# Attention output rows in two halves: six products in place of a step's weighted sums, twice per unit

## The chip, the cores and the metric

The kernel runs on one core of one Trainium2 chip. Its time is the device time of one execution in microseconds. TensorE is called PE below, ScalarE ACT, VectorE DVE, GpSimd POOL, and SP is the engine that issues most DMAs.

## The reference

One transformer block with parallel branches, in float32, over 2048 tokens of 448 features; 16 heads of 28 share one key head and one value head; the hidden layer has 1792 features.

```python
def _A_ref(x, wq, wk, wv, wo):
    q = (x @ wq).reshape(B, S, H, Dh).transpose(0, 2, 1, 3)
    k = x @ wk
    v = x @ wv
    scores = jnp.einsum("bhqd,bkd->bhqk", q, k) * (Dh ** -0.5)
    p = _softmax(scores, axis=-1)
    o = jnp.einsum("bhqk,bkd->bhqd", p, v)
    return o.transpose(0, 2, 1, 3).reshape(B, S, H * Dh) @ wo

def _B_ref(x, w1, b1, w2, b2):
    y = _layernorm(x, axis=-1)
    h = _gelu(jnp.einsum("bsd,df->bsf", y, w1) + b1)
    return jnp.einsum("bsf,fd->bsd", h, w2) + b2

xn = _layernorm(x, axis=-1)
return x + _A_ref(xn, wq, wk, wv, wo) + _B_ref(xn, w1, b1, w2, b2)
```

## The kernel before

The kernel goes through three stages: normalisation and the q, k, v products; the MLP branch, whose result plus `x` and the bias is parked row tile by row tile in DRAM (`ad`); and the attention, which fills the time from about 350 us to the end and is all that the change touches.

**Units and steps.** The attention is cut into 16 units `u`, each 512 queries (chunk `c`) of 4 heads (group `g`), the groups of a chunk one after the other. A unit has 16 key tiles of 128 keys, and its work is laid out in 8 steps `i`. A step holds, in the order that the string `ORDER` spells out:

- 7 or 8 **scores** (`score`, L694 and L695): a 128x512 product on PE into a tile `m` of PSUM, and the exponential from `m` into a tile `p` of SBUF on ACT. `SHARES` deals 60 of them over the 8 steps (8, 8, 8, 7, 7, 7, 7, 8); the first key tile's four blocks come another way (next point).
- in steps 3 to 6, one **maximum product** for the unit after the next (`max_job`, L523 on PE into an `m`, read out by DVE at L530), and one exponential of the next unit's first key tile (`first_exp`, L538 on ACT, from SBUF), which needs a subtraction on DVE first (`first_shift`, L535).
- pieces of the **normalisation** of the last finished unit (`norm_jobs`: copy of `po` at L807, transposes, reciprocal, product, on DVE; a subtraction on POOL), pulled from the stream `side` at the two places `n` of a step.
- at the step's end (`P`) the **weighted sums** of two key tiles (`BURST = 2`): `pv`, L880, four 32-column products per key tile side by side in the array, adding into `po`. They run one step behind the scores; what they use sits in a ring of 12 pairs of `p` tiles.

**The output rows.** When the four groups of a chunk are done, its 512 rows are multiplied with `wo`. That is spread over the next chunk's units: each unit from 4 on does one row tile of 128, `o_part`, in step 5. It is 12 products of 128x448 (4 groups, 3 products each, L767 to L769), one accumulation in one tile `m`, then one addition on DVE to the row that `load_rows_of` fetched from `ad` in step 0 (L772), and the DMA out. In that step the weighted sums are left out, and the step after does four key tiles instead of two:

```python
o_steps = {(u, 5): (u // NG - 1, u % NG) for u in range(NG, NU)}
...
if (u, i) in o_steps:
    o_part(*o_steps[u, i], range(NG))
    continue
for _ in range((BURST if n else 0) * (1 + ((u, i - 1) in o_steps))):
    pv(*pvq.pop(0))
```

**What orders the work.** Every engine runs its instructions in the order in which the program emits them; there is no scheduler. PE therefore cannot start the next scores until a burst of sums or output products is through. The tiles `m` (scores, maximum products, output rows alike) are handed out strictly in turn by `mtile`: seven of them, three from the pool `mp` and four from the pool `ring`. A product into an `m` waits until the tile handed out seven places before has been read. `po` is a single tile. The last unit ends in `pv_last` and `end_jobs`, which the change does not touch.

Of the kernel before, what the change touches and what calls it, by code (L numbers as in the profile page):

```python
# [15 lines left out]
P = 128  # L16
S, D, H, DH, F = 2048, 448, 16, 28, 1792
NT = S // P
CT = 4
NCH = NT // CT  # L20
CW = CT * P
NG = H // 4
# [18 lines left out]
def block_kernel(ctx, tc, x, wq, wk, wv, wo, w1, b1, w2, b2, out):  # L41
    nc = tc.nc
    pe, act, dve, pool = nc.tensor, nc.scalar, nc.vector, nc.gpsimd
# [11 lines left out]
    ov = out[0].rearrange("(p t) d -> p t d", t=NT)  # L55
# [54 lines left out]
    def mtile(shape):  # L110
        if rings:
            given.append(0)
            if len(given) % 7 > 3 or len(given) % 7 == 0:
                return rings[0].tile(shape, F32, name="m")
        return mp.tile(shape, F32, name="m")
# [94 lines left out]
    def bn_end(c, k0=0, n=CT):  # L210
        for k in range(k0, k0 + n):
            dve.bn_aggr(lnp[:, CT * c + k, :], sts[c][:, k, :])
        ts = slice(CT * c + k0, CT * c + k0 + n)
        r = rstd(lnr[:, ts], lnp[:, ts, 1], n)
        next(r)
        yield
        next(r)
        dve.scalar_tensor_tensor(lnb[:, ts], lnp[:, ts, 0], -1.0, lnr[:, ts], op0=ALU.mult, op1=ALU.mult)
        yield
# [9 lines left out]
    def norm_both():  # L229
        dve.tensor_mul(lnq, lnp[:, :, 1], lnr)  # L230
        dve.tensor_mul(lnq, lnq, lnr)
        r = rstd(lnq, lnq, NT)
        next(r)
        yield
        next(r)
        yield
        turned = mtile([NT, P])
        pe.transpose(turned, lnq, ident)
        rows = wp.tile([NT, P], F32, name="rows")
        dve.tensor_copy(rows, turned)  # L240
        nc.scalar.dma_start(second, rows)
        act.activation(warm, one, AF.Tanh)
        yield
# [162 lines left out]
    for c, at in ((2, ((0, 1), (0, 2), (0, 2), (0, 3))), (3, ((1, 0), (1, 1), (1, 2), (1, 3)))):  # L406
        for k in range(CT):
            later(*at[k], lambda t=CT * c + k: bn(t))
        g = bn_end(c)
        for k in range(2):  # L410
            later(c - 1, 0, lambda g=g: next(g), True)
    g = norm_both()
# [12 lines left out]
    NU = len(units)  # L425
    qss, ots = {}, {}
# [43 lines left out]
    def load_q(u, blocks=range(4)):  # L470
        c, g = units[u]
        cols = slice(c * CW, (c + 1) * CW)
        if u < 3 and 0 in blocks:
            qst.append(xt_p.tile([P, 4, CW], F32R, name="xh") if u < 2 else
                       att.tile([P, 4, CW], F32R, name="xh", bufs=1))
            pool.memset(f(qst[u]), 0.0)
        qs = qst[u % 3]
        for b in blocks:
            blk, i = ((1, 0), (2, 0), (0, 1), (3, 1))[b]
            src = qd[i][4 * DH * g:4 * DH * (g + 1), cols].rearrange("(j r) n -> r j n", r=DH)  # L480
            nc.sync.dma_start(f(qs[32 * blk:32 * blk + DH, :, :]), src)
        qss[u] = qs
# [36 lines left out]
    def max_job(u, j):  # L519
        if j == 0:  # L520
            mrs[u] = keep.tile([P, 4 * NT], F32, name="mr2", bufs=2)
        pm = mtile([P, CW])
        pe.matmul(pm, km, qss[u][:, j, :], start=True, stop=True)  # L523
        if u == 0:
            if j == 0:
                lasts.append(f(xl_p.tile([P, 4, CW], F32R, name="xl")))
            tts[u, j] = lasts[0][:, j]
        else:
            tts[u, j] = att.tile([P, CW], F32, name="tt", bufs=5)
        dve.transpose(tts[u, j], pm)  # L530
        dve.tensor_reduce(mrs[u][:, NT * j:NT * j + NT], blocks_of(tts[u, j]), axis=AX.X, op=ALU.max)
# [17 lines left out]
    def shift_jobs(u):  # L549
        for j in range(4):  # L550
            first_shift(u, j)
            yield
            first_exp(u, j)
            yield
            first_back(u, j)
# [130 lines left out]
    def score(u, kt, j):  # L686
        if not halfway:
            p = pair_of()
            halfway.append(p[:, 1])
            p = p[:, 0]  # L690
        else:
            p = halfway.pop()
        s = mtile([P, CW])
        pe.matmul(s, ks[:, kt * P:(kt + 1) * P], qss[u][:, j, :], start=True, stop=True)  # L694
        act.activation(p, s, AF.Exp, scale=SCALE)  # L695
        ps[u, kt, j] = p
# [4 lines left out]
    for n in range(len(mslots) + LAG):  # L701
        c, ft = mslots[n] if n < len(mslots) else (NCH, n - len(mslots))
        if 5 < ft < 10:
            line(CT * MLP_ORDER[c] + ft - 6)
        if 6 < ft < 11:
            a = lines[CT * MLP_ORDER[c] + ft - 7]
# [30 lines left out]
    woh = att.tile([P, NG, D], F32R, name="woh", bufs=1)  # L737
    wol = att.tile([P, NG, D], F32R, name="wol", bufs=1)

    def load_wo():  # L740
        pool.memset(wor, 0.0)
        for j in range(4):
            src = wo.rearrange("(g j d) n -> j d g n", j=4, d=DH)[j]
            nc.sync.dma_start(wor[32 * j + 1:32 * j + 1 + DH, :, :], src)

    def prep_wo(g):
        pool.tensor_scalar(woh[:, g, :], wor[:, g, :], 1.0, 0.0, op0=ALU.mult, op1=ALU.add)
        pool.tensor_sub(wol[:, g, :], wor[:, g, :], f(woh[:, g, :]))

    rows = {}  # L750

    def load_rows_of(c, tiles):
        for k in tiles:
            rows[c, k] = keep.tile([P, D], F32, name="a", bufs=4)
            dve.memset(rows[c, k][0:1, 0:1], 0.0)
            nc.sync.dma_start(rows[c, k], ad[:, CT * c + k, :])
# [3 lines left out]
    def o_part(c, k, gs):  # L760
        if gs[0] == 0:
            parts[c, k] = mtile([P, D])
        po = parts[c, k]
        ts = slice(k * P, (k + 1) * P)
        for g in gs:
            oth, otl = ots[c, g]
            pe.matmul(po, oth[:, ts], woh[:, g, :], start=(g == 0), stop=False)  # L767
            pe.matmul(po, oth[:, ts], wol[:, g, :], start=False, stop=False)  # L768
            pe.matmul(po, otl[:, ts], woh[:, g, :], start=False, stop=(g == NG - 1))  # L769
        if gs[-1] == NG - 1:  # L770
            a = rows[c, k]
            dve.tensor_add(a, a, parts.pop((c, k)))  # L772
            (nc.scalar if k % 2 and c == NCH - 1 else nc.sync).dma_start(ov[:, CT * c + k, :], a)

    def o_jobs(c):
        for k in range(CT):
            o_part(c, k, range(NG))
            yield
# [107 lines left out]
    xside = Stream()  # L886
    pvq = [(u, kt) for u in range(NU) for kt in range(NT)]
    last = NU * NT // 2 - 1
    o_steps = {(u, 5): (u // NG - 1, u % NG) for u in range(NG, NU)}
    for u in range(NU):  # L890
        todo = [(u, kt, j) for kt in range(1 if u else 2, NT) for j in range(4)]
        for i in range(NT // 2):
            n = NT // 2 * u + i
            if n >= last - 1:
                load_rows_of(NCH - 1, (range(CT - 1), [CT - 1])[n - last + 1])
            for v, step in o_steps:
                if v == u and i == 0:
                    load_rows_of(o_steps[v, step][0], [o_steps[v, step][1]])
            if n == 9:
                load_wo()  # L900
            if 12 <= n < 12 + NG:
                prep_wo(n - 12)
            if i == 0 and u + 2 < NU:
                load_q(u + 2)
            jobs = todo[:SHARES[i] if u else 8 * (i > 0)]
            todo = todo[len(jobs):]
            maxima = [(u + 2, i - 3 - (u == 0))] if 3 + (u == 0) <= i < 7 + (u == 0) else []
            if u == 0 and i in (1, 2):
                maxima = [(1, 2 * i - 2), (1, 2 * i - 1)]
            for what in ORDER:  # L910
                if what == "s" and jobs:
                    score(*jobs.pop(0))
                elif what == "M":
                    for v, j in maxima:
                        if v < NU:
                            max_job(v, j)
                elif what in "XY":
                    if what == "X" and i == (2 if u else 3) and u + 1 < NU:
                        xside.add(shift_jobs(u + 1))
                    xside.step()  # L920
                elif what == "e":
                    if i == 7 and u + 2 < NU:
                        load_max(u + 2)
                    if n == 2:
                        load_max(1)
                elif what == "n":
                    side.step()
                elif what == "o":
                    if n == last:
                        o_part(NCH - 1, 0, range(NG - 1))  # L930
                elif what == "P":
                    assert not jobs
                    if (u, i) in o_steps:
                        o_part(*o_steps[u, i], range(NG))
                        continue
                    for _ in range((BURST if n else 0) * (1 + ((u, i - 1) in o_steps))):
                        pv(*pvq.pop(0))
        assert not todo
# [85 lines left out]
```

## Time and profile before

| | us |
|---|---|
| median of 3 runs | 895.28 |
| the three runs | 895.28, 900.3, 891.72 |
| the profiled execution's own time | 891.71 |
| its span | 889.8 |

| engine | busy us (share of the span) | instructions |
|---|---|---|
| PE | 878.8 (99%) | 4914 |
| ACT | 701.9 (79%) | 1334 |
| DVE | 485.7 (55%) | 963 |
| POOL | 73.2 (8%) | 82 |

The granted TensorE clock is 1.000 over the whole span. The shares are averages over stages: the MLP is PE's alone, while in the attention ACT is busy almost all the time as well. Matmuls overlap and their ends are modelled, so PE's 99% does not say whether it has slack; that has to be read from the start times. The profile's count of sums is double the program's: one 32-column float32 product shows as two entries.

### The profile page before, as it was taken

How to read it: one execution, taken by the hardware profiler on the slowest of the kernel's cores; microseconds unless marked ns; L12 is line 12 of the kernel's file. 1: busy time of each engine (PE TensorE's matmuls, PEld its weight loads, DVE VectorE, ACT ScalarE, POOL GpSimd, SP SyncE). 2: the span in 40 equal slices, each digit the busy share in tenths (PEclk: the TensorE clock that was granted, in tenths of full speed). 3: DMA queues.
4: the chain of work that ended last, by engine and by line, in shares of the span. 5: the costliest groups of instructions: out<-in, count | busy, mean ns of one | idle time of the engine just before them, and what ended most of it. 6: DMA issues, size and time to landing. Idle time of an engine off the chain costs nothing.

```text
span 889.8 us, 13236 instructions
## 1 busy us (share of the span) xinstructions
PE 878.8 (99%) x4914; PEld 565.4 (64%) x4914; DVE 485.7 (55%) x963; ACT 701.9 (79%) x1334; POOL 73.2 (8%) x82
## 2 busy tenths in 40 slices
PE   9999999999999999999999999999999999999997
PEld 8777888888888886444444554554554554554555
DVE  6757765656556776654464463463463463463212
ACT  5777564545555457999999999999999999999992
POOL 5450000000000002040000000000000000000000
PEclk9999999999999999999999999999999999999999
DMA  9985232013003004031102202201202201200001
GB/s 293 321 263 173 83 128 83 1 72 118 1 1 105 10 11 125 2 79 43 36 8 53 64 11 53 64 11 53 63 11 53 63 11 53 63 11 13 21 31 66
DMA packets 36297, 60.69 MB, mean 68 GB/s; under 512 B 7782, under 2 KB 23348, under 8 KB 35204
## 3 DMA queue, kind: packets, MB, share of 16 engines
q1 hardware_dynamic: 34644, 58.95, 21.8%
q10 hardware_dynamic: 1584, 0.84, 0.4%
q8 instruction: 40, 0.66, 0.3%
q14 instruction: 29, 0.24, 0.1%
HBM read 39.89 MB, written 18.88 MB: 66 GB/s over the span
## 4 chain that ended last, share of the span: by engine, by line
PE 83%; ACT 8%; DVE 4%; DMA 2%; issue 1%; SPq 0%; ACTq 0%; DVEq 0%
PE m L694 25%; PE po L880 24%; PE ph L178 11%; ACT p L695 5%; PE m L627 4%; PE m L633 4%; PE m L630 4%; PE m L767 2%; PE m L523 2%; PE m L769 1%; PE m L768 1%; PE ph L181 1%; PE ph L183 1%; PE qp L178 1%; DMA raw<-in_B_w_dram 1%
## 5 line engine op out<-in xcount | busy, mean ns | idle before, releaser
L695 ACT ACTIVATE p<-m 128x512 f32<-128x512 f32 x956 | 489.9, 747 | 27.4 <-PE m L694 27.0
L694 PE MATMUL m<-xh,ks 128*128 128x512 f32 x960 | 268.8, 409 | 0.7 <-DVE tt L530 0.3
L694 PEld LDWEIGHTS m<-xh,ks 128*128 128x128 f32 x960 | 174.5, 188 | 139.7 <-ACT p L695 70.8
L880 PE MATMUL po<-p,vs 128*32 128x512 f32 x2016 | 239.9, 598 | 0.0
L880 PEld LDWEIGHTS po<-p,vs 128*32 128x32 f32 x2016 | 53.8, 109 | 119.7 <-issue 119.4
L600 ACT ACTIVATE hz<-hx,b1s 128x512 f32<-128x512 f32 x56 | 40.6, 726 | 101.7 <-DVE hx L597 101.7
L530 DVE STREAM_TRANSPOSE tt<-m 128x512 f32<-128x512 f32 x60 | 42.9, 715 | 94.9 <-PE m L523 94.9
L627 PE MATMUL m<-w2h,hh 128*128 128x448 f32 x224 | 81.9, 366 | 0.0
L633 PE MATMUL m<-w2h,hl 128*128 128x448 f32 x224 | 81.8, 365 | 0.0
L630 PE MATMUL m<-w2l,hh 128*128 128x448 f32 x224 | 81.8, 365 | 0.0
L807 DVE COPY oc<-po 128x512 f32<-128x512 f32 x15 | 10.4, 692 | 120.3 <-PE po L880 120.3
L604 DVE SCALAR_TENSOR_TENSOR hz<-hz,hx 128x512 f32<-128x512 f32 x56 | 38.8, 692 | 52.2 <-ACT hx L601 52.2
L178 PE MATMUL ph<-xh,w1h 128*128 128x512 f32 x159 | 63.1, 397 | 1.8 <-DVE hx L597 1.8
L178 PE MATMUL ph<-xh,w1l 128*128 128x512 f32 x159 | 62.3, 392 | 0.0
L178 PE MATMUL ph<-xl,w1h 128*128 128x512 f32 x159 | 62.3, 392 | 0.0
L822 POOL TENSOR_TENSOR otl<-oc,oth 128x512 fp32r<-128x512 f32 x15 | 24.1, 1608 | 463.5 <-DVE oth L820 272.3
L597 DVE TENSOR_TENSOR hx<-ph,xn 128x512 f32<-128x512 f32 x53 | 36.5, 689 | 39.5 <-PE ph L183 39.3
L538 ACT ACTIVATE tt<-tt 128x512 f32<-128x512 f32 x60 | 53.4, 890 | 0.0
L544 DVE STREAM_TRANSPOSE p<-tt 128x512 f32<-128x512 f32 x60 | 42.1, 702 | 9.4 <-ACT tt L538 9.3
L627 PEld LDWEIGHTS m<-w2h,hh 128*128 128x128 f32 x224 | 42.1, 188 | 5.0
L630 PEld LDWEIGHTS m<-w2l,hh 128*128 128x128 f32 x224 | 42.1, 188 | 4.6
L607 ACT ACTIVATE hz<-hz 128x512 f32<-128x512 f32 x56 | 35.2, 629 | 12.0 <-DVE hz L604 12.0
(173 smaller groups left out, 1040.2 us busy)
## 6 DMA issues: line engine op xcount, KB each, us to landing
xh<-qd SPq DMA_DIRECT2D x64, 224.0 KB
qd<-qe SPq DMA_DIRECT2D x24, 256.0 KB
a<-in_A_x_dram SPq DMA_DIRECT2D x20, 224.0 KB
ad<-a SPq DMA_DIRECT2D x16, 224.0 KB
a<-ad SPq DMA_DIRECT2D x16, 224.0 KB
raw<-in_B_w_dram SPq DMA_DIRECT2D x7, 448.0 KB
out_dram<-a SPq DMA_DIRECT2D x14, 224.0 KB
xd<-xh SPq DMA_DIRECT2D x2, 1024.0 KB
```

The source lines that it names most:

```text
L178: pe.matmul(ps, w, v, start=(n == 0), stop=False)
L530: dve.transpose(tts[u, j], pm)
L538: act.activation(tts[u, j], tts[u, j], AF.Exp, scale=SCALE)
L544: dve.transpose(p0s[u][:, j], tts.pop((u, j)))
L600: act.activation(hz, hx, AF.Square, bias=b1s[:, ft:ft + 1], scale=GELU[0] ** 0.5)
L604: dve.scalar_tensor_tensor(hz, hz, 1.0, hx, op0=ALU.add, op1=ALU.mult)
L627: pe.matmul(m2[k], hh[:, ts], w2h, start=(ft == 0), stop=False)
L630: pe.matmul(m2[k], hh[:, ts], w2l, start=False, stop=False)
L633: pe.matmul(m2[k], hl[:, ts], w2h, start=False, stop=(ft == NF - 1))
L694: pe.matmul(s, ks[:, kt * P:(kt + 1) * P], qss[u][:, j, :], start=True, stop=True)
L695: act.activation(p, s, AF.Exp, scale=SCALE)
L880: pe.matmul(po[32 * j:32 * j + 32, :], vs[:, kt, :], ps.pop((u, kt, j)), start=(kt == 0), stop=(kt == NT - 1))
```

## The change

A row tile's 12 products are done in two halves of six. The first half takes groups 0 and 1 and the place of the sums in step 1; the second takes groups 2 and 3 and the place of the sums in step 5. Each half is an accumulation of its own in its own tile `m`, and each is added to the row in SBUF, so there are two additions on DVE per row tile instead of one. The rows go out after the second. The steps after each, 2 and 6, do four key tiles each.

```diff
+    def o_half(c, k, gs):
+        po = mtile([P, D])
+        ts = slice(k * P, (k + 1) * P)
+        for g in gs:
+            oth, otl = ots[c, g]
+            pe.matmul(po, oth[:, ts], woh[:, g, :], start=(g == gs[0]), stop=False)
+            pe.matmul(po, oth[:, ts], wol[:, g, :], start=False, stop=False)
+            pe.matmul(po, otl[:, ts], woh[:, g, :], start=False, stop=(g == gs[-1]))
+        a = rows[c, k]
+        dve.tensor_add(a, a, po)
+        if gs[-1] == NG - 1:
+            nc.sync.dma_start(ov[:, CT * c + k, :], a)
...
-    o_steps = {(u, 5): (u // NG - 1, u % NG) for u in range(NG, NU)}
+    o_steps = {(u, 4 * h + 1): (u // NG - 1, u % NG, range(2 * h, 2 * h + 2)) for u in range(NG, NU) for h in range(2)}
...
-            for v, step in o_steps:
-                if v == u and i == 0:
-                    load_rows_of(o_steps[v, step][0], [o_steps[v, step][1]])
+            if i == 0 and u >= NG:
+                load_rows_of(u // NG - 1, [u % NG])
...
-                        o_part(*o_steps[u, i], range(NG))
+                        o_half(*o_steps[u, i])
```

The orders of ACT, POOL and SP stay as they are. On PE the two steps 1 and 2 of a unit from 4 on stood like this before (`xh` times `ks` into `m` are the scores, `po` from `p` and `vs` the sums of two key tiles):

```order
L694 MATMUL m<-xh,ks 128x512 x8
L880 MATMUL po<-p_4364,vs 32x512 x4
L880 MATMUL po<-p,vs 32x512 x4
L694 MATMUL m<-xh,ks 128x512 x8
L880 MATMUL po<-p,vs 32x512 x8
```

and stand like this now:

```order
L694 MATMUL m<-xh,ks 128x512 x8
L780 MATMUL m<-woh,oth 128x448
L781 MATMUL m<-wol,oth 128x448
L782 MATMUL m<-woh,otl 128x448
L780 MATMUL m<-woh,oth 128x448
L781 MATMUL m<-wol,oth 128x448
L782 MATMUL m<-woh,otl 128x448
L694 MATMUL m<-xh,ks 128x512 x8
L893 MATMUL po<-p_4364,vs 32x512 x4
L893 MATMUL po<-p,vs 32x512 x12
```

Two key tiles' sums moved behind the second eight scores, where four key tiles now run in one piece, and six products took their place. Step 5 keeps its place and loses six of its twelve products; step 6 keeps its four key tiles.

On DVE the unit's first rows, from the copy of the finished sums to the next unit's first subtraction, were these before (`oc`, `tr`, `rc`: the normalisation; `tt<-tt,mq`: the subtraction that ACT's `first_exp` waits for):

```order
L807 COPY oc<-po 128x512
L786 SCALAR_TENSOR_TENSOR sq,seen<-oc 128x512
L812 STREAM_TRANSPOSE tr<-oc 128x512
L814 RECIPROCAL rc<-tr 128x16
L815 STREAM_TRANSPOSE tr<-rc 128x512
L818 TENSOR_TENSOR oc<-oc,tr 128x512
L820 CAST oth<-oc 128x512
L535 TENSOR_TENSOR tt<-tt,mq 128x512
```

and are these now (`a<-a,m` is the addition of the first half to the row):

```order
L820 COPY oc<-po 128x512
L799 SCALAR_TENSOR_TENSOR sq,seen<-oc 128x512
L825 STREAM_TRANSPOSE tr<-oc 128x512
L827 RECIPROCAL rc<-tr 128x16
L828 STREAM_TRANSPOSE tr<-rc 128x512
L784 TENSOR_TENSOR a<-a,m 128x448
L831 TENSOR_TENSOR oc<-oc,tr 128x512
L833 CAST oth<-oc 128x512
L535 TENSOR_TENSOR tt<-tt,mq 128x512
```

The first half's addition stands between the second transpose and the product of the normalisation; the second half's addition stays where the only one was, behind the last L535 of the unit.

## The prediction

> **What bounds the kernel now.** The page has PE at 99% and ACT at 79% over the span, but the change touches the attention alone, so I asked first for the busy time in stretches: one unit without output rows, two units with them, and unit 14, the last but one. Columns are the stretch, its length, then busy time of PE, PE's weight loads, DVE, ACT and POOL, and the granted clock.
>
> ```profile
> 380.00:411.50 31.50, 31.44 (x196) 14.62 (x192) 16.68 (x34) 31.50 (x66) 9.19 (x9) 1.00 0.30 68
> 502.07:535.57 33.50, 33.50 (x205) 17.08 (x204) 17.03 (x36) 31.54 (x65) 1.67 (x1) 1.00 0.15 43
> 535.57:569.13 33.56, 33.56 (x206) 17.10 (x205) 17.03 (x36) 31.54 (x65) 1.67 (x1) 1.00 0.16 42
> 803.73:836.76 33.03, 32.59 (x201) 16.31 (x200) 9.89 (x18) 31.54 (x64) 1.58 (x1) 1.00 0.08 22
> ```
>
> Without output rows ACT is busy 31.50 of 31.50 us: it sets the pace. With them a unit takes 33.5 us while ACT's work stays 31.54, so ACT stands idle 1.96 us per unit. PE shows as busy throughout, which does not say whether it has slack. So the next view is the order of time, PE's first, for one cycle from step 5 of unit 6 on (start, length, engine, line, count).
>
> ```profile
> 560.63 0.37 PE L767 MATMUL m<-woh,oth 128*128 128x448 f32 x1
> ...
> 563.06 0.39 PE L694 MATMUL m<-xh,ks 128*128 128x512 f32 x1
> 563.28 0.39 PE L523 MATMUL m<-xh,km 128*128 128x512 f32 x1
> 563.51 1.52 PE L694 MATMUL m<-xh,ks 128*128 128x512 f32 x6
> 564.96 3.64 PE L880 MATMUL po<-p,vs 128*32 128x512 f32 x32
> 568.53 2.10 PE L694 MATMUL m<-xh,ks 128*128 128x512 f32 x8
> 570.57 1.92 PE L880 MATMUL po<-p,vs 128*32 128x512 f32 x16
> 572.42 2.14 PE L694 MATMUL m<-xh,ks 128*128 128x512 f32 x8
> 574.49 1.92 PE L880 MATMUL po<-p,vs 128*32 128x512 f32 x16
> 576.34 2.11 PE L694 MATMUL m<-xh,ks 128*128 128x512 f32 x8
> 578.38 1.92 PE L880 MATMUL po<-p,vs 128*32 128x512 f32 x16
> 580.24 2.14 PE L694 MATMUL m<-xh,ks 128*128 128x512 f32 x8
> 582.30 1.92 PE L880 MATMUL po<-p,vs 128*32 128x512 f32 x16
> 584.16 0.50 PE L694 MATMUL m<-xh,ks 128*128 128x512 f32 x1
> 584.49 0.39 PE L523 MATMUL m<-xh,km 128*128 128x512 f32 x1
> 584.72 1.74 PE L694 MATMUL m<-xh,ks 128*128 128x512 f32 x6
> 586.39 1.92 PE L880 MATMUL po<-p,vs 128*32 128x512 f32 x16
> 588.24 0.50 PE L694 MATMUL m<-xh,ks 128*128 128x512 f32 x1
> ```
>
> Read from start to start, each piece has its price. Eight products into `m` behind sums: 568.53 to 570.57, 2.04 us. The same eight behind output products: 563.06 to 564.96, 1.90. Sums of two key tiles: 570.57 to 572.42, 1.85. Of four: 564.96 to 568.53, 3.57. Twelve output products: 560.63 to 563.06, 2.43. With these a unit with output rows needs, on PE alone, seven rows of eight at 2.04, one at 1.90, six bursts at 1.85, one at 3.57 and 2.43: 33.28 us. It takes 33.5. So PE is within 0.2 us per unit of setting the pace itself; ACT's 1.96 us of idleness are not there for the taking.
>
> The next view is ACT in the same stretch, merged and then two narrow looks.
>
> ```profile
> 569.13 15.79 ACT L695 ACTIVATE p<-m 128x512 f32<-128x512 f32 x32 [2.02 <-PE m L694]
> 569.13 0.60 ACT L695 ACTIVATE p<-m 128x512 f32<-128x512 f32 x1 [2.02 <-PE m L694]
> 585.13 0.78 ACT L695 ACTIVATE p<-m 128x512 f32<-128x512 f32 x1
> ACT p L695 <- PE m L694: 17.7, 9, 2.0
> ```
>
> The last row is from the list of waits between 500 and 800 us: nine units, nine waits of about 2.0. There is one per unit, always behind the burst of four. After it the first exponential starts 0.60 us after its score (568.53 to 569.13) and ends 0.60 later: 1.20 from score to free tile. The 32 end at 584.92, so one ends every (584.92 - 569.73)/31 = 0.49 us. From 31.50 = 60 x 0.49 + 4 L538, one L538 takes 0.52.
>
> What holds PE back is in the same rows. The first score of step 3 started at 584.16; its exponential ran from 585.13 to 585.91. The eighth product of that step uses the same tile, seven places on, and came late: the burst behind it starts at 586.39, 2.23 after 584.16 where 2.04 is the rule. Unit 14 shows the rule bare, with PE and ACT:
>
> ```profile
> 826.68 1.32 PE L694 MATMUL m<-xh,ks 128*128 128x512 f32 x5
> 828.44 0.47 PE L767 MATMUL m<-woh,oth 128*128 128x448 f32 x1 [0.44 <-ACT p L695]
> 828.75 0.36 PE L768 MATMUL m<-wol,oth 128*128 128x448 f32 x1
> 827.46 0.93 ACT L695 ACTIVATE p<-m 128x512 f32<-128x512 f32 x1
> ```
>
> The output product is the seventh tile after that step's first score. That score's exponential ends at 827.46 + 0.93 = 828.39, and the product starts at 828.44, 0.05 later. So PE can be seven tiles ahead of ACT and no further, and seven exponentials are 7 x 0.49 = 3.43 us, less than the 3.57 us of a burst of four plus the 1.20 until the next exponential is through. Every burst of four must leave ACT idle, however full the tiles were.
>
> **The change part by part.** The same 12 products and 16 key tiles remain in a unit; what changes is how they are grouped.
>
> *Joins.* Before: six bursts of two, one of four, one output group. After: four of two, two of four, two output groups. PE alone then needs six rows of eight at 2.04, two at 1.90, four at 1.85, two at 3.57 and 12 products for 2.43: 33.01 us, 0.27 less. It is 0.13 for one burst of four in place of two of two (3.70 - 3.57) and 0.14 for eight scores that no longer follow sums. What entering a second output group costs is not bare in any row: between 0, from unit 6, where 560.63 comes at the normal pitch behind the score, and 0.10, the size of the step between 828.44 and 828.75 (0.31) over the next (0.21); I take 0. The Trainium skill, on the page TensorEngine Tiling (Array Packing), section Tiling Modes, says that changing the tiling mode drains TensorE; the trace agrees (2.04 against 1.90), and by that rule alone the change is a gain of 0.27 us per unit.
>
> *Tiles at step 2.* Steps 7, 0 and step 1's scores are untouched, so I keep the times of the rows above. ACT, unbroken since 569.73, ends step 1's first exponential at 569.73 + 16 x 0.49 = 577.57, its eighth at 581.00, and the first of step 2 at 581.49. The first half starts where the sums did, 578.38; six products are half of 2.43, 1.22; step 2's scores start at 579.60 instead of 580.24. The eighth would come 7 x 0.227 us later, 581.19 (1.90 less the 0.32 from the last to the burst). But its tile is that of step 2's first score, free at 581.49 + 0.05 = 581.54: **a wait of 0.35**, and, as in step 3 above (2.23 against 2.04, of which the tile explains half), up to 0.10 more before the burst. I take 0.40: burst at 581.91, next score at 585.48.
>
> *Idle ACT at step 3.* ACT finishes step 2's eight at 581.00 + 8 x 0.49 = 584.92 and L538 at 585.44. The next exponential ends at 585.48 + 1.20 = 586.68 instead of 585.93: 0.75 idle, where there was none.
>
> *Steps 3 to 6.* From 585.48 PE runs two whole steps (3.89 each) and step 5's eight (2.04): second half at 595.30, step 6's eight from 596.52, the eighth at 598.10 if nothing holds it. ACT from 586.68: six more of step 3 (2.94), three L538 (1.56), fourteen of steps 4 and 5 (6.86), then step 6's first: 598.53. The eighth product's tile is that one: free at 598.58, **a wait of 0.48**, with the same allowance 0.53. Burst at 598.95, step 7's first score at 602.52. ACT runs out at 598.53 + 6 x 0.49 = 601.47 and ends its next at 603.72: 1.76 idle. Half of an output group does not shorten that burst, it is still four tiles against six exponentials in hand.
>
> *Sum.* 602.52 - 568.53 = 33.99 per unit against 33.5: **+0.46**, counting by either engine. PE: 33.01 + 0.40 + 0.53 = 33.94. ACT: 31.50 + 0.75 + 1.76 = 34.01. Without the allowances it is +0.36, with 0.10 at both +0.56, and up to 0.10 more for the second entry.
>
> *Units 14 and 15* have no maximum products, 15 no L538 either. They keep the wait of step 2 (0.40) and the gain of 0.27. With fewer products PE gets further ahead, and the idle time behind the one burst of four is shorter:
>
> ```profile
> 836.76 22.83 ACT L695 ACTIVATE p<-m 128x512 f32<-128x512 f32 x46 [1.49 <-PE m L694]
> 863.77 3.54 ACT L695 ACTIVATE p<-m 128x512 f32<-128x512 f32 x7 [0.49 <-PE m L694]
> ```
>
> At 0.13 each I give both together +0.3. Ten units (4 to 13) at 0.46 and these: **+4.9 us**, bounds 3.9 and 6.9.
>
> *What rides along.* On DVE there is one more addition per unit, in front of the normalisation's product:
>
> ```profile
> 563.26 0.62 DVE L772 TENSOR_TENSOR a<-a,m 128x448 f32<-128x448 f32 x1 [1.24 <-PE m L769]
> 578.92 0.71 DVE L815 STREAM_TRANSPOSE tr<-rc 128x512 f32<-128x512 f32 x1
> 579.67 0.69 DVE L818 TENSOR_TENSOR oc<-oc,tr 128x512 f32<-128x512 f32 x1
> 580.74 0.69 DVE L535 TENSOR_TENSOR tt<-tt,mq 128x512 f32<-128x512 f32 x1
> 569.65 0.52 SPq L756 DMA_DIRECT2D a<-ad  x1
> GB/s 293 321 263 173 83 128 83 1 72 118 1 1 105 10 11 125 2 79 43 36 8 53 64 11 53 64 11 53 63 11 53 63 11 53 63 11 13 21 31 66
> ```
>
> Half one's last product ends near 579.39 + 0.37 = 579.76, when DVE is just free of L815 (579.63). The addition runs to 580.4; its tile is wanted by step 2's seventh score at 581.28, so 0.9 us to spare. Behind it L818, L820, L535 slip 0.75, L535 to 582.2; ACT wants it at 584.92, 2.7 to spare. The row is fetched at 569.65, as before, and wanted at 579.8 now; no row gives its landing, and at the 64 GB/s of such slices 224 KB are 3.5 us, an estimate. Cost nothing, all three, while those margins hold. SP, POOL and ACT keep their order; the DMA out stays in step 5. Ring `p`: 24 tiles are in use at the end of step 2, as at the end of step 6 before, and the sums run before the next is needed.
>
> **The rivals.**
>
> *PE's pace alone decides.* If the waits for tiles do not come (ACT frees them sooner than I count), the unit falls to 33.01: 0.46 to 0.5 less, and with the old 0.2 of waits kept 0.27 less, over 12 units 3.2 to 6 us faster, 886 to 888.5. For it: PE's sum is so near the unit's time, and the joins do get fewer. Against: the wait at 828.44 came where this rule puts it. 16%.
>
> *The first half's tile comes free late* (slower). If L815 or the row ends over 0.9 us later than I read, step 2's seventh score waits for it one to one, in every unit from 4 on. DVE's chain ends 0.1 before the addition can start, so there is no more slack in it than those 0.9. At 1.5 us of lateness it is 0.6 per unit, 7.2 us over 12 units, on top of 896.6: 903.8. Against: the chain starts with the sums' end, which does not move, and its rows are alike from unit to unit. 10%.
>
> *The clock.* Products that stop for tiles more often could lose clock: at half rate every unit would gain up to 33 us, hundreds in all. The stretch 380 to 411.5, where ACT sets the pace and PE must wait, shows 1.00 granted, as do all others. The Trainium skill (TensorE: Matmul & The Clock Gate, section A second HAM failure mode: psum-queue depth-cycling) describes that loss; the rows here do not bear it out. 1%.
>
> *No difference*: the moved waits and the joins cancel, 891 to 893. 5%.
>
> **How the numbers follow.** My forecast gets 68%: 891.71 + 4.9 = 896.6 by the profiled execution. That one lies 3.6 under the median of the runs (895.28) and at the lowest of them; on the median it is 900.2. I put the time between, at 898.4. The range: 890.5 takes in no difference and the milder part of the gain on a median like the one shown; 905 is 900.2 plus the upper bounds. Within 1% (about 9 us, what a measurement here tells from nothing) lie the forecast's own +0.55%, most of the gain and no difference: 78%. Slower by more: the late tile, the clock, and the forecast's upper end, 16%. Faster by more: 6%.
>
> **What would show it.** In the changed profile a unit from 5 to 13 lasts 33.9 to 34.1 us; ACT shows two waits per unit, about 0.75 behind step 2 and 1.8 behind step 6, its work still 31.5; the eight products of steps 2 and 6 take 2.3 us from first score to burst instead of 1.90. If those take 1.90, the first rival holds and a unit lasts 33.0; if DVE's first addition ends over 1 us after the last product, the second. A granted clock under 1 would prove the third. I am wrong altogether if one wait per unit remains.

## The result

The changed kernel takes 897.66 us in the median of 22 runs (896.33 to 900.29), the kernel before 892.90 over 22 runs beside it (891.71 to 900.3). The ratio is 1.0054, with a 95% interval of 1.0045 to 1.0064: 4.8 us slower, clear of the noise and within the 1% called no difference above. The forecast was +4.9 us and 898.4. The sum was right. Two of its terms, the waits in steps 2 and 6, were not, and their errors nearly cancelled.

The stretches of the changed kernel's profile, from one end of ACT's idle time behind step 6 to the next (units 5, 6, 9 and 14; columns as before):

```profile
503.64:537.06 33.42, 33.42 (x205) 17.19 (x204) 17.53 (x37) 31.65 (x65) 1.66 (x1) 1.00 0.15 43
537.06:570.72 33.66, 33.66 (x205) 17.19 (x204) 17.53 (x37) 31.64 (x65) 1.66 (x1) 1.00 0.16 42
638.28:672.85 34.57, 34.23 (x206) 17.36 (x205) 17.52 (x37) 31.65 (x65) 1.59 (x1) 1.00 0.15 41
807.84:841.25 33.41, 33.41 (x201) 16.35 (x200) 10.43 (x19) 31.64 (x64) 1.57 (x1) 1.00 0.07 21
```

Before, every unit from 4 to 13 took 33.5 to 33.6. Now they differ, by over a microsecond, though their programs are alike. ACT's work is what it was, and PE counts as busy all the time in two rows that differ by 0.24: the busy share shows nothing of this. ACT's waits do show it (the timeline, rows of units 4, 5, 6, 9 and 10; in brackets the idle time ahead of a row and what ended it):

```profile
487.23 3.04 ACT L695 ACTIVATE p<-m 128x512 f32<-128x512 f32 x6 [2.42 <-PE m L694]
503.64 15.79 ACT L695 ACTIVATE p<-m 128x512 f32<-128x512 f32 x32 [1.06 <-PE m L694]
520.58 3.54 ACT L695 ACTIVATE p<-m 128x512 f32<-128x512 f32 x7 [0.65 <-PE m L694]
537.06 15.79 ACT L695 ACTIVATE p<-m 128x512 f32<-128x512 f32 x32 [1.12 <-PE m L694]
554.24 3.53 ACT L695 ACTIVATE p<-m 128x512 f32<-128x512 f32 x7 [0.89 <-PE m L694]
...
672.85 15.79 ACT L695 ACTIVATE p<-m 128x512 f32<-128x512 f32 x32 [1.71 <-PE m L694]
690.28 3.54 ACT L695 ACTIVATE p<-m 128x512 f32<-128x512 f32 x7 [1.15 <-PE m L694]
```

There are two per unit, as forecast. Behind step 2 it is 0.65 in unit 5, 0.89 in unit 6, 2.42 in unit 4; behind step 6 it is 1.06 to 1.13 in most units and 1.71 in two. PE's timeline: step 2 of unit 4, steps 1 to 3 and 6 of unit 5, and the end of step 6 of unit 9:

```profile
478.90 2.04 PE L694 MATMUL m<-xh,ks 128*128 128x512 f32 x6
482.39 0.73 PE L694 MATMUL m<-xh,ks 128*128 128x512 f32 x2 [1.46 <-ACT p L695]
...
510.92 2.11 PE L694 MATMUL m<-xh,ks 128*128 128x512 f32 x8
514.08 2.47 PE L694 MATMUL m<-xh,ks 128*128 128x512 f32 x8
516.48 3.64 PE L893 MATMUL po<-p,vs 128*32 128x512 f32 x32
520.04 0.50 PE L694 MATMUL m<-xh,ks 128*128 128x512 f32 x1
...
531.02 0.39 PE L694 MATMUL m<-xh,ks 128*128 128x512 f32 x1
531.25 0.39 PE L523 MATMUL m<-xh,km 128*128 128x512 f32 x1
531.48 1.54 PE L694 MATMUL m<-xh,ks 128*128 128x512 f32 x6
532.95 3.64 PE L893 MATMUL po<-p,vs 128*32 128x512 f32 x32
...
668.25 0.49 PE L694 MATMUL m<-xh,ks 128*128 128x512 f32 x1 [0.34 <-ACT p L695]
668.68 1.91 PE L893 MATMUL po<-p,vs 128*32 128x512 f32 x14
```

In unit 5 the eight scores of step 2 take 516.48 - 514.08 = 2.40 us instead of 1.90 without a wait; those of step 6 take 532.95 - 531.02 = 1.93, no wait at all. In unit 4 the seventh score of step 2 is held up for 1.46 us, and in unit 9 the eighth product of step 6 waits. From the start of each unit's first score to the next's (worked out from the start times), the change adds 1.6 us in unit 4, 2.6 in units 5 to 13 together, 0.3 in unit 14 and 0.1 in unit 15: 4.6. The rest of the 5.9 between the two profiled spans lies behind the last addition, which ends at 889.8 against 885.2.

The two numbers that recur below are the length of the run of eight products into `m` in step 2 and in step 6, from its first start to the start of the burst behind it: 1.90 to 1.95 without a wait, and more by what PE waited.

### The profile page after: what moved, and what is told of

Its sections match the earlier page's. It is cut to its first block, busy times and chain, and to the rows that moved or that the text cites. A ratio compares the mean times of both kernels' runs of the same rounds, so it can differ in the third digit from the quotient of the medians.

```text
span 895.7 us, 13250 instructions
## 1 busy us (share of the span) xinstructions
PE 882.7 (99%) x4914; PEld 568.4 (63%) x4914; DVE 492.1 (55%) x975; ACT 703.0 (78%) x1334; POOL 73.2 (8%) x82
## 4 chain that ended last, share of the span: by engine, by line
PE 78%; ACT 14%; DVE 4%; DMA 2%; issue 1%; SPq 0%; ACTq 0%; POOL 0%; POOLq 0%; DVEq 0%
PE m L694 23%; PE po L893 22%; PE ph L178 11%; ACT p L695 10%; PE m L627 4%; PE m L633 4%; PE m L630 4%; PE m L523 1%; PE ph L181 1%; PE ph L183 1%; PE m L396 1%; PE m L780 1%; PE m L782 1%; PE m L781 1%; DMA qd<-qe 1%
## 5 line engine op out<-in xcount | busy, mean ns | idle before, releaser
L695 ACT ACTIVATE p<-m 128x512 f32<-128x512 f32 x956 | 483.0, 703 | 30.9 <-PE m L694 30.4
L694 PE MATMUL m<-xh,ks 128*128 128x512 f32 x960 | 274.7, 410 | 2.8 <-ACT p L695 2.3
L893 PE MATMUL po<-p,vs 128*32 128x512 f32 x2016 | 237.4, 597 | 0.0
L538 ACT ACTIVATE tt<-tt 128x512 f32<-128x512 f32 x60 | 47.2, 786 | 0.0
```

Source lines behind the costliest of these rows:

```text
L538: act.activation(tts[u, j], tts[u, j], AF.Exp, scale=SCALE)
L893: pe.matmul(po[32 * j:32 * j + 32, :], vs[:, kt, :], ps.pop((u, kt, j)), start=(kt == 0), stop=(kt == NT - 1))
```

## The experiments

The first four ran together; the kernel before was at 893.17 beside them.

**Bursts of three.** The loss could be ACT's idleness behind bursts of four, or PE's waits ahead of them. Without bursts of four the two give different times.

```diff
-                    for _ in range((BURST if n else 0) * (1 + ((u, i - 1) in o_steps))):
+                    late = (u, i - 1) in o_steps or (u, i - 2) in o_steps
+                    for _ in range((BURST if n else 0) + late):
```

> Both halves as in the change, but the two key tiles left out in step 1 (and 5) are caught up as three tiles in step 2 and three in step 3 (6 and 7), so no burst of four is left. Theory 'tiles' (PE loses only where a score stands before an m tile that ACT has not read; the short output group lets PE run into that limit at the end of steps 2 and 6, whatever burst follows): PE's products and joins are the same as in the changed kernel, the eight scores of step 2 still take 2.4 to 2.9 us, and the time stays at the changed kernel's 897.7, within 1.5. Rival 'bursts' (the loss is ACT standing idle behind each burst of four): with no burst over 2.71 us seven exponentials cover it, the idle time goes, and a unit falls to PE's 33.0: about 888, 5 us under the kernel before.

Measured: 897.77, ratio 1.0051 (1.0033 to 1.0069), the changed kernel's time. The idle time did not go, it was split up:

```profile
510.06 11.87 ACT L695 ACTIVATE p<-m 128x512 f32<-128x512 f32 x24 [0.73 <-PE m L694]
526.99 3.54 ACT L695 ACTIVATE p<-m 128x512 f32<-128x512 f32 x7 [0.61 <-PE m L694]
538.74 4.03 ACT L695 ACTIVATE p<-m 128x512 f32<-128x512 f32 x8 [0.31 <-PE m L694]
543.49 11.87 ACT L695 ACTIVATE p<-m 128x512 f32<-128x512 f32 x24 [0.72 <-PE m L694]
```

Unit 5 takes 543.49 - 510.06 = 33.43 (33.42 in the changed kernel), units 5 to 13 vary from 33.4 to 34.4 as they do there, and step 2's run takes 2.37 to 2.86. The rival falls: ACT's idle time is the difference between PE's unit and ACT's work, wherever it shows up, and is no loss of its own.

**Tiles strictly in turn.** The forecast counted on seven tiles handed out in turn. They come from two pools, and each pool hands out what it counts as free.

```diff
-    rings, given = [], []
+    rings, given, turns = [], [], []
...
-                return rings[0].tile(shape, F32, name="m")
-        return mp.tile(shape, F32, name="m")
+                return rings[0].tile(shape, F32, name=f"r{len(given) % 7}", bufs=1)
+        turns.append(0)
+        return mp.tile(shape, F32, name=f"m{len(turns) % 3}", bufs=1)
```

> The changed kernel with the seven m tiles as seven single tiles taken strictly in turn, in place of two pools of three and four that hand out whichever tile they count free first. Nothing else changes. Theory 'slots' (in the changed kernel a score sometimes gets the tile of the sixth or even the third product before it, since the output row's tile is freed late): step 2's eight scores take 2.3 to 2.4 us in every unit, where they now vary from 2.40 to 2.93 and 4.16 in unit 4; step 6's take 2.4 in every unit, where now most take 1.93; unit 4's extra 1.7 us goes. Sum 0.5 less per unit at step 2 on average 0.35, 0.4 more at step 6, 1.7 less in unit 4: 896 to 897, 1 to 2 under the changed kernel. Rival (strict turns as I counted in the prediction were already what happens, and the spread has another cause, such as DVE): nothing changes, 897.7, and the spread stays.

Measured: 898.76, ratio 1.0073 (1.0055 to 1.0090). The spread is gone, every unit is like the next, and unit 4's extra wait with it:

```profile
503.87 0.60 ACT L696 ACTIVATE p<-r 128x512 f32<-128x512 f32 x1 [1.71 <-PE r L695]
520.82 1.09 ACT L696 ACTIVATE p<-r 128x512 f32<-128x512 f32 x2 [0.65 <-PE r L695]
537.88 0.60 ACT L696 ACTIVATE p<-m 128x512 f32<-128x512 f32 x1 [1.71 <-PE m L695]
554.82 1.09 ACT L696 ACTIVATE p<-m 128x512 f32<-128x512 f32 x2 [0.65 <-PE m L695]
```

A unit takes 34.01, the runs of steps 2 and 6 are 2.43 to 2.47 in every unit from 5 to 13, and the idle times, from end to end less one exponential as the prediction counts them, 0.76 and 1.82. The prediction's own numbers were 33.99, 2.30 and 2.43, 0.75 and 1.76. So the order of the tiles makes the spread, as expected; the sum was a miss, 2 us over what I had set down, because the runs I had expected at 2.3 to 2.4 are 2.45, and unit 4 starts 1.3 us later than in the changed kernel's profile.

**Sums stay in step 1.** Half of the change: the first six products come behind step 1's two key tiles instead of in their place.

```diff
                         o_half(*o_steps[u, i])
-                        continue
+                        if i == 5:
+                            continue
-                    for _ in range((BURST if n else 0) * (1 + ((u, i - 1) in o_steps))):
+                    for _ in range((BURST if n else 0) * (1 + (i == 6 and (u, 5) in o_steps))):
```

> Half of the change: the first half of six products is done in step 1 behind the two key tiles' sums, which stay there; step 2 has two key tiles as in the kernel before; step 5 and 6 as in the change (six products, then four key tiles). Theory 'tiles': no wait at step 2, since the run before it got longer, not shorter; PE's sum is 33.28 as before (seven bursts), and step 6 keeps its small wait: a unit takes 33.4 to 33.6, so 892 to 894, no difference from the kernel before. ACT idles once behind step 1 or 2 by about 0.7 and once behind step 6 by about 1.2. Rival (the second tile and second addition, or the halving itself, cost the 4.8 us): stays at 897 to 898.

Measured: 897.29, ratio 1.0052 (1.0037 to 1.0067). A miss. Step 2's wait went as expected (2.04 in units 5 to 7, the length of a run behind sums), but step 6's grew: 2.28 in units 5 and 6, 2.05 in 7 and 8, 2.82 in 9 and 10. A unit from 5 to 13 takes 33.59 to 34.36, with PE's sum back at 33.28 since no burst is saved. I had carried the changed kernel's 1.93 over to a unit in which ACT no longer idles behind a burst of four in step 2. The trace shows that ACT is further behind when step 6 comes: in units 5 to 13 the exponential of step 5's last score ends 1.33 us after step 6's first score starts, where it is 0.97 to 1.04 in the changed kernel. In units 5 and 6 the fifth score of step 6 starts 1.39 us behind the first, right after that exponential. Unit 4 keeps a long wait as well: its step 2 takes 3.32, where it is 4.16 in the changed kernel.

**Nine and three.** Same steps, but three groups in step 1 and one in step 5.

```diff
-    o_steps = {(u, 4 * h + 1): (u // NG - 1, u % NG, range(2 * h, 2 * h + 2)) for u in range(NG, NU) for h in range(2)}
+    o_steps = {(u, 4 * h + 1): (u // NG - 1, u % NG, range(3 * h, 3 + h)) for u in range(NG, NU) for h in range(2)}
```

> The change with nine products (three groups) in step 1 and three in step 5. Nine take 1.82 us, as long as the two key tiles' sums whose place they have (1.85). Theory 'tiles': step 2's scores meet their tiles ready, their run falls from 2.4 to 2.9 towards 1.95 to 2.3, 0.6 less; step 6's run comes 0.6 earlier and waits up to 0.6 more, 1.93 becoming 2.2 to 2.5: the sum per unit falls by 0 to 0.4, 894 to 898. ACT idles 1.3 to 1.5 behind step 2 and 0.5 to 0.7 less than now behind step 6. Rival 'PE's pace alone': same products, same joins, no change at all in any run of scores, 897.7.

Measured: 896.72, ratio 1.0043 (1.0029 to 1.0058). The wait moves from one end to the other:

```profile
514.55 1.98 PE L694 MATMUL m<-xh,ks 128*128 128x512 f32 x8
516.46 2.35 PE L893 MATMUL po<-p,vs 128*32 128x512 f32 x20
...
530.64 0.39 PE L523 MATMUL m<-xh,km 128*128 128x512 f32 x1
530.87 2.13 PE L694 MATMUL m<-xh,ks 128*128 128x512 f32 x6
532.93 1.06 PE L893 MATMUL po<-p,vs 128*32 128x512 f32 x8
```

In unit 5 step 2's run is 516.46 - 514.55 = 1.91, where it was 2.40; in step 6 the products behind the first score alone now take 2.29 (532.93 - 530.64), where they took 1.70 (532.95 - 531.25). What a longer first group gives PE, the shorter second one takes back. With PE's pace alone nothing would have moved.

The next four ran together, the kernel before at 892.62.

**The halving alone.** Two tiles and two additions, both in step 5.

```diff
-    o_steps = {(u, 4 * h + 1): (u // NG - 1, u % NG, range(2 * h, 2 * h + 2)) for u in range(NG, NU) for h in range(2)}
+    o_steps = {(u, 5): (u // NG - 1, u % NG) for u in range(NG, NU)}
...
-                        o_half(*o_steps[u, i])
+                        for h in range(2):
+                            o_half(*o_steps[u, i], range(2 * h, 2 * h + 2))
```

> The halving alone: both halves, each with its own tile and its own addition on DVE, in step 5 where the kernel before does its twelve products; the sums of step 1 stay in step 1, one burst of four in step 6. Theory 'tiles': twelve products are 2.43 us in one piece again, the joins and the runs between them are those of the kernel before, so no new wait: a unit takes 33.5, 893, within 1.5 of the kernel before. Rival (the second tile and the second addition cost the time): 896 to 898.

Measured: 892.54, ratio 1.0005 (0.9995 to 1.0015), units of 33.5. The second tile and the second addition cost nothing that can be measured.

**The kernel before, strictly in turn.** The same edit to `mtile` as above.

> The kernel before with the seven m tiles taken strictly in turn. Theory 'tiles': its only waits for tiles are the 0.15 to 0.2 us at step 3, and its output row's tile is seldom handed out of turn, so it stays as it is: 33.4 to 33.6 per unit, 893, within 1. Then strict turns against strict turns, the change is worth 898.8 against 893: 0.5 us per unit, as the prediction counted it. Rival (strict turns cost by themselves, and that is why the changed kernel with them is the slowest so far): 894.5 or more.

Measured: 894.09, ratio 1.0015 (1.0007 to 1.0024), between the two expectations. Its units take 33.57 each, 0.5 us more over units 5 to 13 together. Where the rest of the 1.5 us lies is not shown: in its profile unit 4 starts 3.4 us later than in the kernel before, but the two profiled executions also differ in the granted clock ahead of the attention. The same stretch in this kernel's profile and in that of the kernel before (the clock is the third number from the end):

```profile
84.90:88.30 3.40, 3.40 (x10) 2.68 (x9) 1.75 (x3) 1.44 (x3) 0.00 (x0) 0.50 0.20 75
84.90:88.30 3.40, 3.40 (x18) 3.04 (x17) 2.35 (x5) 2.36 (x5) 0.00 (x0) 1.00 0.04 16
```

PE starts 10 products in it instead of 18. Strict against strict, the change costs 34.0 - 33.57 = 0.43 us per unit.

**Six tiles.** The changed kernel, strict, with a ring of three.

```diff
-            if len(given) % 7 > 3 or len(given) % 7 == 0:
+            if len(given) % 6 > 3 or len(given) % 6 == 0:
...
-    rings.append(ctx.enter_context(tc.tile_pool(name="ring", bufs=4, space=PSUM)))
+    rings.append(ctx.enter_context(tc.tile_pool(name="ring", bufs=3, space=PSUM)))
```

> The changed kernel with strict turns and six m tiles in place of seven. Theory 'tiles': the waits at the end of steps 2 and 6 are set by the exponential of the score so many tiles before; one tile less is one exponential more, 0.49: the runs of 2.45 become 2.9 to 3.0, and ACT's idle times 0.76 and 1.82 become 1.25 and 2.3: a unit from 5 to 13 takes 34.9 to 35.1 instead of 34.0. With small waits in the other units the whole is 908 to 914. Rival 'PE's pace': the number of tiles does not matter to PE's products and joins; at most 1 us per unit less than that, 899 to 901.

Measured: 911.3, ratio 1.0205 (1.0190 to 1.0221); a unit's stretch, and ACT's two waits in it:

```profile
506.40:541.14 34.74, 34.48 (x205) 17.03 (x204) 17.56 (x37) 31.71 (x64) 1.66 (x1) 1.00 0.15 41
```

```profile
506.40 0.60 ACT L696 ACTIVATE p<-m 128x512 f32<-128x512 f32 x1 [1.88 <-PE m L695]
523.91 0.60 ACT L696 ACTIVATE p<-r 128x512 f32<-128x512 f32 x1 [1.15 <-PE r L695]
```

Behind step 2 ACT idles 0.5 more (1.15 against 0.65), one exponential for one tile, as counted; behind step 6 only 0.17 more. PE's timeline of step 6 in unit 5 shows why:

```profile
534.38 0.39 PE L695 MATMUL m<-xh,ks 128*128 128x512 f32 x1
...
536.38 0.73 PE L695 MATMUL m<-xh,ks 128*128 128x512 f32 x2 [0.26 <-ACT p L696]
537.04 1.05 PE L894 MATMUL po<-p,vs 128*32 128x512 f32 x6
```

With six tiles in turn it is the seventh of the step's eight products that needs the tile of its first score, 2.00 us after that score's start, and the eighth gets the maximum product's tile, which DVE has long emptied. With seven tiles the eighth product waited in the same way. So the run grows by one product, from 2.45 to 2.66 - 2.70, and not by a whole exponential. A unit takes 34.74 instead of the expected 34.9 to 35.1. PE's pace does not explain any of it.

**Whole rows, bursts of three.** The kernel before with the catch-up edit of the first experiment.

> The kernel before (twelve products in step 5, one tile), but the two key tiles left out there are caught up as three in step 6 and three in step 7, so that it has no burst of four. Theory 'tiles': PE's products and joins are the same, and PE has no wait for tiles there to lose, so the idle time of ACT behind step 6 (2.06) shrinks and turns up again behind step 7 and later: 893, within 1. Rival 'bursts': 1 to 1.5 us per unit less, 876 to 881.

Measured: 892.1, ratio 0.9992 (0.9983 to 1.0001); units of 33.47. No burst of four and the same time, as the first experiment showed from the other side.

The last two ran together, the kernel before at 893.08. Both put L538, which ACT does from SBUF, behind the first score of its step:

```diff
-ORDER = "YnsMssnsXsossseP"
+ORDER = "nsYMssnsXsossseP"
```

**In the strict changed kernel:**

> The changed kernel with strict turns, and the exponential of the next unit's first key tile (L538) behind the first score's exponential of its step instead of ahead of it. Theory 'tiles', counted through: from step 3's first exponential, which comes out of idleness, to step 6's first, ACT still has three L538 to do, so the tile that step 6's eighth product waits for is free no sooner: the run of 2.45 stays in steps 2 and 6, a unit stays at 34.0 and the time at that of the strict kernel, 898.8 within 1.5; only ACT's idle times change places, 0.76 to 1.3 behind step 2 and 1.82 to 1.3 behind step 6. Rival (the step's own L538 is what makes step 6 wait): the run of step 6 falls to 1.95, a unit to 33.5, 893 to 894.

Measured: 900.31, ratio 1.0076 (1.0055 to 1.0098). Units of 34.00, runs of 2.45 in both steps, and the idle times 1.26 and 1.31: as counted through, to the hundredth in the unit. The whole time is at the upper edge of what was expected (898.8 within 1.5), over four runs.

**In the kernel before with bursts of three:**

> The kernel before with its catch-up as three and three tiles, and L538 behind the first score's exponential of its step. Theory 'tiles': here ACT comes into step 3 without a pause, so its first score's tile is free 0.5 earlier and the only wait of PE in the unit goes: the run of step 3 falls from 2.18 to 2.05, a unit from 33.47 to 33.3, ten or eleven units: 890.5, about 2 under the kernel before. Rival (PE's waits at step 3 are not for that tile): 892, as with the threes alone.

Measured: 889.06, ratio 0.9962 (0.9947 to 0.9977): **faster than both**. Two units of it, and PE's timeline of step 3:

```profile
507.52:540.84 33.32, 33.32 (x205) 17.16 (x204) 17.03 (x36) 31.75 (x64) 1.67 (x1) 1.00 0.14 40
540.84:574.16 33.32, 33.32 (x205) 17.16 (x204) 17.04 (x36) 31.75 (x64) 1.67 (x1) 1.00 0.16 44
```

```profile
518.70 0.50 PE L694 MATMUL m<-xh,ks 128*128 128x512 f32 x1
519.04 0.40 PE L523 MATMUL m<-xh,km 128*128 128x512 f32 x1
519.28 1.56 PE L694 MATMUL m<-xh,ks 128*128 128x512 f32 x6
520.76 1.92 PE L880 MATMUL po<-p,vs 128*32 128x512 f32 x16
```

Step 3's run is 520.76 - 518.70 = 2.06, where the kernel before has 2.18 to 2.25. PE now waits nowhere in these units, and 33.32 is the sum of its pieces (33.28). It gains 4 us where 2 were expected. The units give 0.2 each and unit 14 another 0.6, since its output group no longer waits (the run ahead of it takes 1.76 against 2.33): some 2.5 in all. Between the lowest runs of the two kernels the difference is 2.4 (888.54 against 890.91), so the rest may be no more than the spread of 6 and 11 runs; that stays open, and what the later L538 gives without the bursts of three was not tried.

## Why the prediction was right, and where it was not

*What bounds the kernel* held: PE, within 0.2 us per unit, and tiles that ACT has not read. The last experiment shows it from below: PE's pieces laid end to end take 33.3, and no less while the joins stay. Six tiles show it from above.

*Joins.* 33.01 us were forecast for PE alone. Unit 5 of the changed kernel, at 33.42 with 0.5 us of waits in step 2, is at 32.92 without them. The gain of a saved burst is there, and a second output group costs nothing to enter.

*Tiles at step 2 and at steps 3 to 6.* Here the step failed, in one premise: "its tile is that of step 2's first score" and its counterpart in step 6 assume that tiles are handed out in turn, which the description of the kernel also says. They are not. Where the tiles are taken in turn, the two waits and the unit come out as counted (34.0, 0.76, 1.82). In the kernel as it is, the output row's tile is passed over in some units, and scores behind it get a tile sooner than the seventh place. The waits in the trace show it, since DVE empties the row's tile and ACT those of scores: in unit 5 the seventh score of step 2 waits for DVE, so it has the row's tile; in unit 6 the eighth does; in unit 4 none of the eight does. In unit 4 the seventh waited for ACT:

```profile
479.61 4.69 ACT L695 ACTIVATE p<-m 128x512 f32<-128x512 f32 x9
```

and DVE's addition of the row was through before:

```profile
479.10 0.62 DVE L784 TENSOR_TENSOR a<-a,m 128x448 f32<-128x448 f32 x1
```

The nine exponentials are step 1's last and step 2's eight; they end at 484.30, so the fourth score's ends four times 0.49 earlier, at 482.34, and the seventh score starts at 482.39. It had been given the tile of the fourth, three places back. In step 6 it is the other way round: the maximum product's tile, which DVE empties at once, comes to the last score in most units, and the wait of 0.53 is not there. Over units 5 to 13 step 2 cost 0.73 on the average where 0.40 was forecast, step 6 0.13 where 0.53 was; unit 4 cost 1.6 instead of 0.46. That the sum was right to 0.1 us owes something to chance: units 5 to 13 came out some 1.5 us shorter together than forecast, and unit 4 1.2 longer. The forecast time of 898.4 was set between two levels of the kernel before; over 22 runs that kernel came to 892.90, and with 4.9 added that is 897.8. By the prediction's own signs, two waits per unit came and ACT's work stayed (31.65), but of the units from 5 to 13, at 33.4 to 34.6 between ACT's pauses, only unit 8 lay within 33.9 to 34.1, and step 6's run was 1.93 to 1.94 in seven of the nine, which had been named as the sign of the first rival.

*What rides along* held: the addition in unit 4 ends at 479.72, 1.0 us after the last product's start, as in every other unit and as counted (579.39 to 580.4), and in the attention's units from 4 on no L538 starts after a pause of ACT.

*The rivals.* PE's pace alone is refuted by the waits that came, and by six tiles. The late tile gave the right place, step 2's seventh score, and the wrong reason: in unit 4 the score was held up for 1.46 us although the addition was through. The clock stayed at 1.00 in every unit of the attention that is quoted. It was not at 1.00 throughout: in four profiles (the changed kernel with bursts of three, the kernel before strictly in turn, and the last two) it stood at 0.50 for 3.4 us near 85 us, before the attention, with the change and without it, and in every profile it falls to 0.50 in the last microseconds. Those four have means of 0.996 and 0.997 over the span, the other eight 0.998 to 1.000. The units' lengths, on which the argument rests, do not contain that stretch. The loss by cycling through PSUM that the Trainium skill describes (TensorE: Matmul & The Clock Gate, section A second HAM failure mode: psum-queue depth-cycling) did not come with waits of 0.2 to 1.5 us in every unit.

## What to carry to other kernels

When one engine fills a ring of tiles and another empties it, a shorter piece of other work between two runs of filling need not save its length: the filler runs into the ring's end and waits there. Here the waits took more than the joins had saved, 0.43 us per unit with tiles strictly in turn. Count where the filler stands, tile by tile, before counting the emptier's idle time, which is only the difference of the two. And look up which tile each product really gets; the two pools of three and four tiles did not behave as one ring of seven.

## What was not expected of the hardware

An exponential's recorded length is no price. In an unbroken run it grows, 0.60 us just after a pause (569.13 in the kernel before) and 0.78 sixteen microseconds later (585.13), while the ends stay 0.49 apart on the average (the prediction works this out from 569.73 and 584.92).
